# Where a weight tile's conversion keeps its scratch, and which PSUM bank takes seven of its differences

## The chip, the cores and the metric

The kernel runs on one core of a Trainium2 chip. The metric is the device time of one execution in microseconds (us): 1154.68 us is the median of three runs of the kernel before.

## The reference

Three stages follow one another, all in fp32:

```
for t in range(768):                       # 4 batches x 8 heads, head size 48
    S = a_n[t] * S + outer(k[t], v[t])     # complex decay a_n, real k and v
    y[t] = q[t] @ real(S)
x = y as [3072 tokens, 384]
x = relu(x @ w_in)**2 @ w_out                            # 384 -> 2048 -> 384
x = (silu(x @ w_gate) * (x @ w_val)) @ w_out2            # 384 -> 1536 -> 384
```

The weights come in fp32. The kernel splits every weight, and every activation that meets one, into a high part of TensorE's fp32r kind and the difference to it, and adds three products of such parts.

## The kernel before

**Stages.** The 768 steps are cut into six chunks of 128 steps (512 tokens). Chunk n goes through `attention(n)`, which forms the recurrence in closed form: `elem` does elementwise work (mostly VectorE and ScalarE), `mat` does small matmuls on TensorE, by four groups of two heads. Its result lies in `xf`, and `moe1(n)` multiplies it: for each of 16 column tiles i of 128, nine matmuls into `h` (by `w1t[i]`), ScalarE makes u = relu squared, `gh` and `gl` are its two parts, and two tiles later nine matmuls (`down`) add into three accumulators `acc0` to `acc2` (by `w2t[i]`). Meanwhile `attention(n+1)` runs. After chunk 5, `moe2` runs for all chunks.

**Weights of the first product.** `prep1` (line 815) converts 32 weight tiles, number j = 0 to 31, by turns of w_in (`wc`) and w_out (`wr`). A tile is read into a staging buffer `wst` (four of them, the slots w28 to w31), and three VectorE instructions build its high and low bits in an int32 scratch tile `wt` of 128x384 (`wsplit`, line 739). ScalarE casts `wt` into the first half of the weight tile. The second half is the difference: for j < 16 TensorE forms it in a PSUM tile `pw` (one matmul of `wt`, one of the first half with a negative identity) and ScalarE copies it out; from 16 on VectorE subtracts. Two ScalarE passes over `wst` look for values out of bounds and end the use of that staging buffer.

**Where things lie.** The 32 weight tiles have slots w0 to w31, tile j in slot j. While the first chunk's attention runs, slots 12 to 27 hold its inputs and intermediate tiles. The scratch `wt` takes a buffer of the ring `u` (three buffers), which `moe1` uses for its u too. PSUM has eight banks: three with the name `ps`, two with `h`, and one each for `acc0`, `acc1`, `acc2`. The first chunk's `mat` goes round seven of them, all but `acc2`. `pw` takes `acc2` while the flag `nc.later` is set, and a `ps` bank otherwise.

**Order.** All instructions from attention to the end are recorded first. `Plan.arrange` (line 172) then plays through them with estimated durations: whenever an engine is free it takes the ready instruction of lowest rank, which is the place in the recording (plus 1000 while `nc.later` is set). Buffers of one tag are given out in the order of their tiles' first recorded use, and a tile that isn't next in that order can't begin. The resulting list is issued (line 306, so nearly all instructions carry that line), each engine working strictly down its own list. In the recording, `drain` mixes generators by weights: during `attention(0)` one step of `prep1` goes in for every 25 steps of attention, with `later` = 1000 (line 1028); then `behind` puts two conversions ahead of each tile i of `moe1(0)` (line 1031), mixed with `attention(1)`. `attention(0)` has some 97 steps, so three conversions (j = 0 to 2) are recorded within it; j = 3 and 4 come right behind it, then u of tile 0, then j = 5 and 6, then u of tile 1, and so on.

Of the kernel before, what the change touches and what calls it, by code (L numbers as in the profile page):

```python
# [11 lines left out]
I32 = mybir.dt.int32  # L12
# [296 lines left out]
class Kern:  # L309
# [426 lines left out]
                yield  # L736


    def wsplit(self, dst, src, early=False, pe=None):

        nc = self.nc
        lo, hi = src[:, :, 0], src[:, :, 1]
        if early:
            t = self.mp.tile([128, 512], I32, name="wt", tag="u", bufs=self.NU)[:, 0:384]
        else:
            t = self.e2.tile([128, 384], I32, name="wt", tag="smk", bufs=self.NSMK)
        nc.vector.tensor_scalar(out=t, in0=hi, scalar1=3, scalar2=0x3FFFFFF8,
                                op0=ALU.logical_shift_left, op1=ALU.bitwise_and)
        nc.vector.scalar_tensor_tensor(out=t, in0=hi, scalar=-0x40000000, in1=t,
                                       op0=ALU.bitwise_and, op1=ALU.bitwise_or)  # L750
        nc.vector.scalar_tensor_tensor(out=t, in0=lo, scalar=29, in1=t,
                                       op0=ALU.logical_shift_right, op1=ALU.bitwise_or)
        x = t.bitcast(F32)
        if self.guard:
            nc.vector.tensor_scalar(out=hi, in0=hi, scalar1=0x7FFFFFFF, scalar2=None, op0=ALU.bitwise_and)
            nc.vector.scalar_tensor_tensor(out=x, in0=hi.bitcast(F32), scalar=WLOW, in1=x, op0=ALU.is_ge, op1=ALU.mult)
        nc.scalar.copy(dst[:, 0], x)
        if pe:
            pw = (self.ps if pe == "ps" else self.psa).tile([128, 384], F32, name="pw", tag=pe)
            nc.tensor.matmul(pw, self.ident, x, start=True, stop=False)  # L760
            nc.tensor.matmul(pw, self.nident, dst[:, 0], start=False, stop=True)
            nc.scalar.copy(dst[:, 1], pw)
        else:
            nc.vector.tensor_tensor(out=dst[:, 1], in0=x, in1=dst[:, 0].bitcast(F32), op=ALU.subtract)
        if not self.guard:
            hi = hi.bitcast(F32)
            nc.scalar.activation(out=hi, in_=hi, func=AF.Square, accum_out=self.flag(1))
            nc.scalar.activation(out=hi, in_=hi, func=AF.Relu, scale=-1.0, bias=self.wlow2, accum_out=self.flag(2))
# [39 lines left out]

        self.convert("wr", self.read_row(src, i), i, dst)

    def convert(self, name, st, i, dst, early=False, pe=None):
        dst[i] = t = self.wtile(name)
        self.wsplit(t.rearrange("p x k f -> p x (k f)"), st, early, pe)

    def prep1(self, ahead=0):

        self.w1t, self.w2t = {}, {}
        todo = [x for i in range(self.F1 // 128) for x in (
            (self.read_col, self.w1, i, "wc", self.w1t), (self.read_row, self.w2, i, "wr", self.w2t))]
        own = len(todo) - ahead  # L820
        read = []
        for j in range(-1, len(todo)):
            while len(read) < min(len(todo), j + max(ahead, 1)):
                f, src, i, _, _ = todo[len(read)]
                read.append(f(src, i, own + len(read) % ahead if len(read) < own and ahead else None))
            if j >= 0:
                _, _, i, name, dst = todo[j]
                self.convert(name, read[j], i, dst, ahead > 0, self.nc.later and "acc2" or "ps" if 0 < ahead and j < self.BYPE else None)
            yield

    def prep2(self):
# [377 lines left out]
```

## Time and profile before

| | |
|---|---|
| median of three runs | 1154.68 us (1154.52 to 1156.37) |
| the profiled execution: its time | 1152.95 us |
| its span, first to last instruction | 1150.8 us |
| mean granted TensorE clock | 0.984 |
| PE (matmul) busy | 1064.3 us, 92% |
| PEld (weight load) busy | 898.7 us, 78% |
| VectorE (DVE) busy | 707.5 us, 61% |
| ScalarE (ACT) busy | 617.3 us, 54% |

PE is TensorE's matmul stream, PEld its weight loads, SPq the queue that issues nearly all transfers. A row of the timeline has the start and duration in us, the engine, the line, the operation, output <- inputs, and in brackets how long the engine had been idle before it and what ended that. The span is 2.15 us shorter than the profiled execution's time, and that time is 1.73 us under the median.

### The profile page before, as it was taken

The page shows a single profiled execution, that of the slowest core. Times are in us where ns is not written, and L with a number is a line of the kernel's source. Part 1 is how long each engine was busy: PE and PEld are TensorE (multiplying, and loading weights), DVE is VectorE, ACT ScalarE, POOL GpSimd, SP SyncE. Part 2 cuts the span into 40 slices and gives each one's busy share as a digit, 9 for nine tenths or more (in the row PEclk, how much of TensorE's full clock was granted, in tenths as well). Part 3 has the DMA queues.
Part 4 walks back from the last instruction along what each step waited for, and adds up shares of the span by engine and source line. Part 5 has one row for each costly group of instructions (what it writes and reads, how often), then busy time and mean ns, then how long its engine had stood idle before and what let it go on. Part 6 is the DMA issues. An engine that isn't in the chain of part 4 may idle for free.

```text
span 1150.8 us, 16440 instructions
## 1 busy us (share of the span) xinstructions
PE 1064.3 (92%) x5890; PEld 898.7 (78%) x5890; DVE 707.5 (61%) x1485; ACT 617.3 (54%) x1334; POOL 0.9 (0%) x7
## 2 busy tenths in 40 slices
PE   2449679999999999999999999999999999999997
PEld 0347467887888888888887887888888888888886
DVE  7987999799699799789748893232232222322221
ACT  6558689966676776766759994222122222221221
POOL 0000000000000000000000000000000000000000
PEclk9969989999999999999999999999999999999998
DMA  5453346412621531531446441010010100000000
GB/s 141 129 144 96 110 149 195 110 43 75 162 68 49 153 90 50 141 85 54 137 119 190 150 148 56 1 56 1 1 55 1 55 1 1 28 1 1 28 1 31
DMA packets 102491, 89.25 MB, mean 78 GB/s; under 512 B 35073, under 2 KB 90369, under 8 KB 102401
## 3 DMA queue, kind: packets, MB, share of 16 engines
q1 hardware_dynamic: 102080, 87.93, 26.3%
q8 instruction: 48, 0.79, 0.3%
q14 instruction: 43, 0.34, 0.1%
q10 hardware_dynamic: 320, 0.20, 0.1%
HBM read 64.49 MB, written 18.87 MB: 72 GB/s over the span
## 4 chain that ended last, share of the span: by engine, by line
PE 77%; ACT 10%; DVE 7%; DMA 2%; SPq 2%; issue 2%; ACTq 0%; DVEq 0%
PE acc L306 25%; PE pg L306 13%; PE pv L306 13%; PE h L306 13%; PE py L306 4%; ACT wst L306 4%; PE pt L306 3%; PE sc L306 3%; PE pu L306 3%; SPq L306 2%; ACT u L306 1%; DVE AB L306 1%; DMA kn<-scr 1%; DVE an L306 1%; DVE wt L306 1%
## 5 line engine op out<-in xcount | busy, mean ns | idle before, releaser
L306 ACT CAST gh<-u 128x512 fp32r<-128x512 f32 x168 | 103.7, 618 | 244.4 <-PE acc L306 217.0
L306 PE MATMUL acc<-gh,wr 128*128 128x512 f32 x576 | 198.2, 400 | 4.2 <-ACT gh L306 4.1
L306 PE MATMUL h<-xh,wc 128*128 128x512 f32 x576 | 196.2, 397 | 2.7 <-ACT u L306 1.9
L306 DVE TENSOR_TENSOR gl<-u,gh 128x512 fp32r<-128x512 f32 x168 | 115.3, 688 | 126.2 <-ACT gh L306 125.7
L306 DVE TENSOR_TENSOR u<-pv,u 128x512 f32<-128x512 f32 x72 | 49.8, 692 | 204.9 <-PE pv L306 203.8
L306 PE MATMUL acc<-wr,gh 128*128 128x384 f32 x576 | 146.7, 335 | 0.0
L306 PE MATMUL pg<-xh,wc 128*128 128x512 f32 x396 | 134.8, 394 | 1.1 <-ACT xh L306 1.1
L306 PE MATMUL pv<-xh,wc 128*128 128x512 f32 x396 | 133.8, 392 | 1.3 <-ACT u L306 1.3
L306 PEld LDWEIGHTS acc<-gh,wr 128*128 128x128 f32 x576 | 107.8, 189 | 28.0 <-ACT gh L306 6.0
L306 PEld LDWEIGHTS h<-xh,wc 128*128 128x128 f32 x576 | 108.1, 189 | 26.5 <-ACT u L306 2.7
L306 PE MATMUL acc<-gl,wr 128*128 128x512 f32 x288 | 114.6, 398 | 0.2 <-DVE gl L306 0.2
L306 PE MATMUL h<-xl,wc 128*128 128x512 f32 x288 | 113.2, 393 | 0.0
L306 PEld LDWEIGHTS acc<-wr,gh 128*128 128x128 f32 x576 | 105.1, 188 | 5.2
L306 ACT ACTIVATE u<-pg 128x512 f32<-128x512 f32 x72 | 43.1, 599 | 104.7 <-PE pg L306 104.7
L306 PE MATMUL acc<-wr,gl 128*128 128x384 f32 x288 | 96.6, 335 | 0.0
L306 PEld LDWEIGHTS pv<-xh,wc 128*128 128x128 f32 x396 | 74.3, 188 | 18.3 <-ACT u L306 1.7
L306 PEld LDWEIGHTS pg<-xh,wc 128*128 128x128 f32 x396 | 74.3, 188 | 16.2 <-ACT xh L306 1.5
L306 ACT ACTIVATE u<-h 128x512 f32<-128x512 f32 x96 | 56.6, 591 | 47.3 <-PE h L306 41.7
L306 PE MATMUL pg<-xl,wc 128*128 128x512 f32 x198 | 78.2, 395 | 0.1
L306 PE MATMUL pv<-xl,wc 128*128 128x512 f32 x198 | 77.8, 393 | 0.0
L306 DVE SCALAR_TENSOR_TENSOR wt<-wst,wt 128x384 int32<-128x384 int32 x136 | 73.7, 552 | 1.6
L306 DVE TENSOR_TENSOR AB<-an 128x768 f32<-128x768 f32 x72 | 68.4, 950 | 0.7
(132 smaller groups left out, 1738.3 us busy)
## 6 DMA issues: line engine op xcount, KB each, us to landing
wst<-in_moe_w_out_dram SPq DMA_DIRECT2D x28, 384.0 KB, 3.3
scr<-ks SPq DMA_DIRECT2D x24, 384.0 KB, 2.5
kn<-scr SPq DMA_DIRECT2D x24, 384.0 KB, 3.7
wst<-in_moe_w_in_dram SPq DMA_DIRECT2D x16, 384.0 KB, 3.7
in<-in_k_dram SPq DMA_DIRECT2D x96, 48.0 KB, 1.9
in<-in_q_dram SPq DMA_DIRECT2D x96, 48.0 KB, 2.0
vt<-in_v_dram SPq DMA_DIRECT2D x48, 96.0 KB, 2.8
x2d<-x SPq DMA_DIRECT2D x18, 256.0 KB, 2.1
```

The source lines that it names most:

```text
L306: o.call(*o.args, **o.kw)
```

## The change

The scratch `wt` of tile j moves out of the ring `u` into the slot of the tile two further on (j + 2), for j + 2 below 28; the last six stay in the ring. `pw` of the first seven tiles takes the bank `acc2`, where before only those recorded under `later` did; tiles 7 to 15 stay with `ps`. `prep2`, which converts the later weights, passes no `early` and keeps its own scratch.

```diff
-    def wsplit(self, dst, src, early=False, pe=None):
+    def wsplit(self, dst, src, early=None, pe=None):
         nc = self.nc
         lo, hi = src[:, :, 0], src[:, :, 1]
-        if early:
+        if early is None:
+            t = self.e2.tile([128, 384], I32, name="wt", tag="smk", bufs=self.NSMK)
+        elif early < self.WBUFS - self.READ:
+
+            t = self.slot("wt", [128, 384], I32, early)
+        else:
             t = self.mp.tile([128, 512], I32, name="wt", tag="u", bufs=self.NU)[:, 0:384]
-        else:
-            t = self.e2.tile([128, 384], I32, name="wt", tag="smk", bufs=self.NSMK)
...
-    def convert(self, name, st, i, dst, early=False, pe=None):
+    def convert(self, name, st, i, dst, early=None, pe=None):
...
-                self.convert(name, read[j], i, dst, ahead > 0, self.nc.later and "acc2" or "ps" if 0 < ahead and j < self.BYPE else None)
+                self.convert(name, read[j], i, dst, j + 2 if ahead else None, "acc2" if j < 7 else "ps" if 0 < ahead and j < self.BYPE else None)
```

## Rows read from the trace of the kernel before

**Rows 1.** The page's parts 1 and 2: engines, then 40 slices in tenths.

```profile
PE 1064.3 (92%) x5890; PEld 898.7 (78%) x5890; DVE 707.5 (61%) x1485; ACT 617.3 (54%) x1334; POOL 0.9 (0%) x7
...
PE   2449679999999999999999999999999999999997
...
DVE  7987999799699799789748893232232222322221
```

**Rows 2.** Busy time by stretch of the span; the first row names the columns.

```profile
core 0: us, PE busy (x) PEld busy (x) DVE busy (x) ACT busy (x) POOL busy (x), PEclk, DMA share, GB/s
...
60.00:96.00 36.00, 21.00 (x164) 18.26 (x158) 29.03 (x74) 22.82 (x53) 0.00 (x0) 0.72 0.49 133
96.00:114.00 18.00, 16.94 (x68) 12.27 (x67) 15.88 (x34) 16.56 (x41) 0.00 (x0) 1.00 0.35 86
114.00:150.00 36.00, 23.30 (x84) 16.09 (x82) 35.90 (x90) 24.60 (x64) 0.00 (x0) 0.87 0.31 92
150.00:168.00 18.00, 14.81 (x85) 11.50 (x84) 16.85 (x40) 14.20 (x37) 0.00 (x0) 0.97 0.60 184
168.00:216.00 48.00, 47.58 (x375) 38.74 (x374) 41.85 (x91) 46.30 (x121) 0.00 (x0) 1.00 0.57 166
```

**Rows 3.** Waits of PE, 90 to 160 us, then 160 to 232: total, times, longest.

```profile
PE pw L306 <- DVE wt L306: 7.4, 3, 3.4
PE acc L306 <- ACT gh L306: 4.0, 2, 3.7
PE h L306 <- ACT u L306: 1.9, 2, 1.6
...
PE py L306 <- DVE rho L306: 2.9, 1, 2.9
```

**Rows 4.** Timeline: conversions 3 and 4, u of tile 0, conversions 5 and 6.

```profile
49.98 0.35 DVE L306 TENSOR_SCALAR wt<-wst 128x384 int32<-128x384 int32 x1
...
56.58 0.31 DVE L306 TENSOR_SCALAR wt<-wst 128x384 int32<-128x384 int32 x1
...
95.58 0.88 PE L306 MATMUL pw<-wt,ident 128*128 128x384 f32 x2
...
102.29 0.60 ACT L306 ACTIVATE u<-h 128x512 f32<-128x512 f32 x1 [0.62 <-PE h L306]
102.39 0.62 DVE L306 TENSOR_SCALAR wt<-wst 128x384 int32<-128x384 int32 x2
```

**Rows 5.** Stretches of tile pw: stretch, length, PE, PEld, ACT busy (count).

```profile
35.00:95.50 60.50, 0.00 (x0) 0.00 (x0) 0.00 (x0) 0.83 0.47 138
95.50:114.00 18.50, 5.79 (x17) 3.30 (x18) 2.33 (x5) 1.00 0.35 87
```

**Rows 6.** A stretch of tile wt: PE, PEld, DVE, ACT busy (count).

```profile
95.50:114.00 18.50, 4.75 (x12) 2.17 (x12) 5.00 (x12) 2.04 (x4) 1.00 0.35 87
```

**Rows 7.** Timeline: the longest two waits of DVE between 60 and 96 us.

```profile
82.34 0.56 DVE L306 SCALAR_TENSOR_TENSOR b<-sq,b 128x384 f32<-128x384 f32 x1 [0.95 <-ACT b L306]
...
89.57 0.55 DVE L306 TENSOR_TENSOR state<-pu,rho 96x384 f32<-96x384 f32 x1 [2.65 <-PE pu L306]
```

**Rows 8.** Timeline: a matmul into pw, u of tile 5 and the accumulation behind it.

```profile
136.84 0.81 PE L306 MATMUL pw<-wt,ident 128*128 128x384 f32 x2
...
139.54 0.58 ACT L306 ACTIVATE u<-h 128x512 f32<-128x512 f32 x1
...
141.48 1.65 PE L306 MATMUL acc<-gh,wr 128*128 128x512 f32 x3 [3.66 <-ACT gh L306]
```

**Rows 9.** Timeline: weight loads for pw of conversions 1 and 2, in bank acc2.

```profile
16.17 0.50 PEld L306 LDWEIGHTS pw<-wt,ident 128*128 128x128 f32 x2 [1.40 <-ACT wc L306]
...
18.99 0.50 PEld L306 LDWEIGHTS pw<-wt,ident 128*128 128x128 f32 x2 [1.67 <-ACT wr L306]
```

**Rows 10.** The SP queue's waits, 0 to 300 us: total, times, longest.

```profile
SPq L306 <- ACT wst L306: 32.7, 20, 5.0
```

**Rows 11.** The chain of waits where moe1(0) ends and moe1(1) begins.

```profile
222.79 6.12 PE acc L306 x27
228.91 6.15 PE h L306 x27
```

**Rows 12.** Timeline: the last transfers into xf of chunk 1.

```profile
215.90 1.15 SPq L306 DMA_DIRECT2D xf<-ys  x2
```

## The prediction

> **What bounds the kernel now.** I read the 40 slices first, then busy time by stretch, then who PE waited for, then the timeline where it waited. The slices show two kernels in one [rows 1]: from the seventh slice on PE is at nine tenths or more nearly to the end, and over the span it is busy 92%; in the first six slices it is not, and there VectorE is at seven to nine tenths. So only the first 170 us can give anything back by better order; whatever PE loses there is lost to the end, since all later work queues behind it. By stretch [rows 2]: from 60 to 96 us the first chunk's attention runs, PE is busy 21.0 of 36 us and DVE 29.0. From 96 to 114 moe1(0) starts, and PE is busy 16.9 of 18. From 114 to 150 PE is busy only 23.3 of 36, DVE 35.9: VectorE is the bound. From 150 to 168 PE has 14.8 of 18, and from 168 to 216 it has 47.6 of 48. PE's idle time from 96 to 168 is thus 1.1 + 12.7 + 3.2 = 17.0 us, and the waits name its causes [rows 3]: 7.4 us for scratch tiles that VectorE had not built, 4.0 for gh, 1.9 for u, 2.9 for rho of the attention.
>
> **Why the conversions are late.** Two orders of buffers hold them. Conversion 3 is built on VectorE from 49.98 us and conversion 4 from 56.58, but no matmul into pw runs between 35 and 95.5 us [rows 4, 5]; the first comes at 95.58. Its bank is of `ps`, given out in order of recording, and all of attention(0) is recorded ahead of it. Until then the scratch tiles 3 and 4 hold two of the ring's three buffers. Behind them in the ring stands u of tile 0, which begins at 102.29 when moe1(0) has its first `h`; conversions 5 and 6 come behind that u, and start 0.1 us after it, at 102.39. From there each pair of conversions is tied to the u before it, and the u to the pair before it. One case shows what that costs: u of tile 5 comes behind scratch 14 in the ring; a matmul on a scratch tile still runs at 136.84, u begins at 139.54, and PE has then sat 3.66 us waiting for the gh made from it [rows 8].
>
> **The change part by part.**
>
> *The bank.* pw of conversions 3 to 6 goes to acc2, which attention(0) never uses; no instruction is added or removed. Conversions 3 and 4 can then end some 40 us earlier, and 5 and 6 needn't wait for ps. Of PE's work, 17 matmuls into pw, 5.79 us, lie between 95.5 and 114 us [rows 5]; at three per conversion that is 5.79 / 17 x 3 = 1.02 us each, so four of them move 4.1 us into a stretch where PE has 15 us idle [rows 2]. That is worth 4.1 us if PE is the bound right after 96 and nothing if VectorE is. As VectorE is the bound from 114 on, I take nothing for it in the sum, and keep 4.1 for the upper end.
>
> *One bank for four.* The four follow one another in a single bank, so each waits for ScalarE to empty the one before. The rows of conversions 1 and 2 show that wait on PEld: 1.40 and 1.67 us [rows 9]. Queued behind such a wait on PE are attention(0)'s transposes and score matmuls, and ScalarE and VectorE wait for those. Three such waits are 3 x 1.67 = 5.0 us of PE at most; PE's 15 us of idle time hides them, and I take 0, with 5.0 as the far end if they fall just ahead of a transpose that is due.
> The Trainium skill says in Perfetto Trace Analysis, section Matmuls, that independent matmul groups should go round different PSUM banks, so that emptying one overlaps the next group's matmuls. These two rows agree that without it a group waits; by that rule the bank costs up to the 5.0 us, by the stretch's idle time it costs nothing.
>
> *The scratch.* wt of conversions 0 to 25 leaves the ring. What goes is the tie to u: conversions 5 and on can be built as soon as their read has landed and VectorE has a free moment, and u has three buffers to itself. What is added is a new order in the slots: the weight tile j + 2 can't be written before scratch j is done with. Scratch 10 and on lie in slots that attention(0) uses, so they wait for its qs, ks and kn; those end by about 96 us. So up to seven conversions (3 to 9) could be built ahead of 96 us, in place of two. What limits them is VectorE and the four staging buffers. Four conversions (5 to 8) cost VectorE 12 instructions and 5.00 us, which now lie between 95.5 and 114 us [rows 6]. Between 60 and 96 us VectorE has 36.00 - 29.03 = 7.0 us idle [rows 2], 0.95 and 2.65 us of it in two waits [rows 7]. So those 5.0 us fit. The planner puts them there by rank, behind all attention(0) work, but an engine can't break off an instruction; I take 1.0 us of delay of attention(0)'s end for that (two instructions of 0.5 us at bad moments; bounds 0 and 5.0, if every one of them delays the chain). In the DVE-bound stretch 5.0 us less of VectorE work means that PE's needs are met 5.0 us earlier.
>
> *The stalls by the ring.* 3.66 us for gh [rows 8] and 1.6 us for u [rows 3] are waits in which u came late: 5.3 us. With u free of the scratch they can go, but VectorE, busy 35.9 of 36 us there, is the next to be late, with gl and the scratch tiles. I take half, 2.65 us (bounds 0 and 5.3).
>
> *The handover.* moe1(1) takes over at 228.91 behind 6.12 us of accumulation [rows 11], and the last transfers of its input are issued at 215.90 [rows 12]. They need some microseconds to land and be split; still, about 8 us of slack stand between attention(1)'s end and PE's need. A gain of under 8 us passes even if attention(1) ends no earlier; VectorE has 48.0 - 41.9 = 6.1 us idle from 168 to 216 [rows 2] to catch up in. From there PE is the bound, and I carry the gain to the end undiminished.
>
> *Sum.* 5.0 - 1.0 + 2.65 = 6.65 us. On the profiled execution: 1152.95 - 6.65 = 1146.3 us; its time is 1.73 us under the median, so on the scale of the medians 1154.68 - 6.65 = 1148.0 us.
>
> **The rivals.**
>
> *VectorE's work is only moved (no change).* From 60 to 168 us VectorE is the chain; its gaps are waits inside that chain, and every conversion put into one could delay attention(0) by as much as it saves later. Then 5.0 - 5.0, and the freed u finds VectorE late: 1154.7, give or take 2 us. Against it: 2.65 of the 7.0 us are one wait for PE, in which four instructions fit [rows 7].
> The Trainium skill, Perfetto Trace Analysis, section Identifying the Most-Contended Engine, says to work on the engine with the highest occupancy; by that alone PE, at 92%, is the one, the change takes no instruction from it, and the time stays 1154.7. The trace agrees from 168 us on, and not from 114 to 150, where VectorE is at 35.9 of 36.
>
> *The reads stand in the way (slower).* A conversion that ends early lets the next read into its staging buffer, and the SP queue works in order: it already waits 32.7 us in 20 times for ScalarE to finish with wst, 5.0 at the longest [rows 10]. If a read of tiles 9 to 12 stands there ahead of the last groups' ks, kn or ys transfers, attention(0) ends later by that wait. Two waits of 5.0 us against the 6.65 gained give 3.4 us slower, 1158. It decides from the point where the waits ahead of those transfers exceed 6.65 us. Against it: the planner counts the read's readiness before it places it.
>
> *All stalls go (more).* If conversions stay ahead of moe1(0) for good, the 17.0 us of PE's idle time [rows 2] shrink to little, and the 4.1 us of pw count too: 21.1 us at most. Half to all of that gives 1133.6 to 1144. For it: VectorE has 7.0 us idle before 96 and 6.1 after 168. Against it: it has 0.1 between 114 and 150, and attention(1) must end earlier by what exceeds the 8 us of slack.
>
> **How the numbers follow.** Forecast, 3 to 10.5 us gained: 0.55, at 1148.0, own range 1144 to 1152. More than that: 0.15. No change: 0.16. Reads in the way or another slowing: 0.14. A measurement of this kernel tells about 0.2% (2.3 us) from no change. Faster 0.70, same 0.16, slower 0.14. The range for 8 in 10 goes from 1138, within the rival with more, to 1157, within the slower one.
>
> **What the trace after would show.** Right: pw matmuls of conversions 3 to 6 and scratch tiles 5 to 8 ahead of 95 us; attention(0)'s last transfer into xf within 2 us of where it was; PE's idle time from 96 to 168 at about 10 us in place of 17; PE's start of moe1(1) 5 to 9 us earlier and no new gap after it. Wrong: VectorE as idle before 96 as now; moe1(0)'s first h later by as much as the stalls shrink; SP waits for wst ahead of ks, kn or ys; or a new wait of PE at 220 us for xf of chunk 1.

## The result, and the profile after

The change is faster: 1144.95 us, the median of six runs (1144.47 to 1146.38), against 1155.48 for the kernel before on the same chip (six runs, 1153.10 to 1156.85). The ratio is 0.9913, with a 95% interval of 0.9900 to 0.9926, or 10.0 us (the two medians differ by 10.5). The forecast was 1148.0 us and 6.65 us of gain, the range 1138 to 1157: sign and mechanism hold, the gain was half as large again. Between the two profiled executions it is 1152.95 - 1144.72 = 8.2 us; the profiled execution of before lies 2.5 us under the median of its runs, that of after 0.2. The traces can explain only those 8.2.

The page of after, engines and slices, answers to [rows 1]:

```profile
PE 1067.2 (93%) x5890; PEld 899.9 (79%) x5890; DVE 705.8 (62%) x1485; ACT 619.3 (54%) x1334; POOL 1.0 (0%) x7
...
PE   2458979999999999999999999999999999999997
...
DVE  6998999799789789789658883232232222322221
```

No instruction went or came: the counts are those of before, and over the span no engine is busier by more than 3 us. What changed is when the work is done. Busy time by stretch, in the columns of [rows 2] (length, PE, PEld, DVE, ACT, POOL, granted clock, DMA share, GB/s):

```profile
60.00:96.00 36.00, 23.92 (x151) 17.70 (x151) 32.35 (x85) 28.91 (x74) 0.00 (x0) 0.72 0.52 141
96.00:114.00 18.00, 14.83 (x68) 10.64 (x68) 17.43 (x37) 15.64 (x37) 0.00 (x0) 0.81 0.54 146
114.00:150.00 36.00, 30.15 (x131) 24.12 (x129) 35.19 (x89) 27.49 (x67) 0.00 (x0) 0.95 0.33 95
150.00:168.00 18.00, 15.65 (x89) 12.71 (x90) 17.73 (x41) 13.55 (x33) 0.00 (x0) 0.81 0.57 170
168.00:216.00 48.00, 47.60 (x368) 38.66 (x367) 41.11 (x87) 45.99 (x117) 0.00 (x0) 1.00 0.55 157
```

VectorE's idle time ahead of 96 us fell from 7.0 to 3.65 us. PE's idle time from 96 to 168 fell from 17.0 to 3.2 + 5.8 + 2.4 = 11.4 us; it fell by 6.9 us between 114 and 150, where VectorE was the bound and still is, and grew by 2.1 ahead of 114. The waits of PE from 96 to 240 us (total, times, longest) show what is left:

```profile
PE pt L306 <- DVE ks L306: 8.2, 1, 8.2
PE h L306 <- ACT xh L306: 2.4, 1, 2.4
PE h L306 <- ACT u L306: 0.8, 1, 0.8
PE h L306 <- DVE xl L306: 0.7, 1, 0.7
```

All the causes of [rows 3] are gone: the 7.4 us for scratch, 4.0 for gh, 2.9 for rho, and most of the u. Two waits have come in their place, 8.2 us for ks, the scaled k of attention(1), and 2.4 for xh, the high part of moe1(0)'s input (0.8 before). The timeline of after, in order of time (start, duration, engine, line, operation, idle time before it):

```profile
57.94 0.81 PE L306 MATMUL pw<-wt,ident 128*128 128x384 f32 x2
...
62.03 0.35 DVE L306 TENSOR_SCALAR wt<-wst 128x384 int32<-128x384 int32 x1
...
64.74 1.65 PE L306 MATMUL pw<-wt,ident 128*128 128x384 f32 x2 [1.56 <-ACT wr L306]
...
67.28 1.65 PE L306 MATMUL pw<-wt,ident 128*128 128x384 f32 x2 [0.57 <-ACT wc L306]
...
77.36 0.62 DVE L306 TENSOR_SCALAR wt<-wst 128x384 int32<-128x384 int32 x2
...
97.97 0.57 ACT L306 ACTIVATE ys<-py 48x512 f32<-48x512 f32 x1
...
101.72 0.52 SPq L306 DMA_DIRECT2D xf<-ys  x1
...
104.60 0.62 ACT L306 CAST xh<-xf 128x512 fp32r<-128x512 f32 x1 [0.19 <-DMA xf<-ys]
...
105.27 0.93 PE L306 MATMUL h<-xh,wc 128*128 128x512 f32 x2 [2.43 <-ACT xh L306]
...
152.35 1.09 PE L306 MATMUL pt<-ident,ks 128*96 128x128 f32 x4 [8.20 <-DVE ks L306]
...
221.81 0.39 PE L306 MATMUL h<-xh,wc 128*128 128x512 f32 x1
```

The pw of conversion 3 now runs at 57.94 us, not at 95.58 [rows 4]; conversion 5 begins on VectorE at 62.03, not at 102.39, 7 and 8 at 77.36, and 9 at 83.99. In one bank, two of the pw groups wait for ScalarE, 1.56 and 0.57 us, as in [rows 9]. Then the bill: the last two ys of attention(0), 0.7 us apart, come 2.7 us later than before (the first of them at 97.97 for 95.25; that one is meant by "the last ys" below), the last transfer into xf is issued at 101.72 (before, the last two from 97.04 within 1.16 us, so the last at about 97.6), and the last cast into xh 4.5 us later (104.60 for 100.12). moe1(1) begins at 221.81, for 228.75 before. Two rows on the tiles pw (PE, PEld, ACT busy) and wt (PE, PEld, DVE, ACT busy) of after:

```profile
35.00:95.00 60.00, 7.10 (x12) 3.01 (x12) 1.92 (x4) 0.83 0.47 137
...
35.00:96.00 61.00, 5.72 (x8) 1.81 (x8) 9.89 (x21) 3.04 (x6) 0.83 0.48 139
```

Twelve matmuls into pw, four differences, where [rows 5] has none. 21 VectorE instructions on scratch are seven conversions, 3 to 9, where before there were two in 2.86 us: five more, and 7.0 us of VectorE's time moved ahead.

The gain can be balanced on PE from 60 us to the start of moe1(1). The two long rows of before, and then those of after:

```profile
96.00:168.00 72.00, 55.05 (x234) 39.86 (x233) 68.63 (x162) 55.36 (x138) 0.00 (x0) 0.93 0.39 113
168.00:228.75 60.75, 60.33 (x431) 49.25 (x430) 51.23 (x108) 58.21 (x147) 0.00 (x0) 1.00 0.55 154
```

```profile
96.00:168.00 72.00, 60.63 (x286) 47.46 (x286) 70.36 (x164) 56.69 (x134) 0.00 (x0) 0.88 0.44 126
168.00:221.81 53.81, 53.41 (x394) 43.45 (x392) 45.38 (x95) 51.43 (x129) 0.00 (x0) 1.00 0.53 151
```

With the 15.0 and 12.1 us of idle time ahead of 96, PE idles 15.0 + 16.95 + 0.42 = 32.4 us before and 12.1 + 11.37 + 0.40 = 23.9 after, 8.5 less; it is busy 136.4 and 138.0 us, 1.6 more at a lower clock. 8.5 - 1.6 is the 6.9 us by which moe1(1) starts earlier. Chunk 1 adds 2.0 (its idle time falls from 3.0 to 0.9 us). In the chain of waits moe1(2) and moe1(4) then begin here, against 330.61 and 525.54 before:

```profile
321.65 6.12 PE h L306 x27
...
517.38 6.12 PE h L306 x27
```

That is 9.0 and 8.2 us earlier, and 8.2 it is at the end.

### The profile page after: what moved, and what is told of

The parts are those of the page before. It is cut to its first block, busy times and chain, and to the rows that moved or that the text cites. A ratio compares the mean times of both kernels' runs of the same rounds, so it can differ in the third digit from the quotient of the medians.

```text
span 1142.6 us, 16426 instructions
## 1 busy us (share of the span) xinstructions
PE 1067.2 (93%) x5890; PEld 899.9 (79%) x5890; DVE 705.8 (62%) x1485; ACT 619.3 (54%) x1334; POOL 1.0 (0%) x7
## 4 chain that ended last, share of the span: by engine, by line
PE 79%; ACT 9%; DVE 6%; DMA 2%; SPq 2%; issue 1%; ACTq 0%; DVEq 0%
PE acc L306 26%; PE h L306 13%; PE pg L306 13%; PE pv L306 13%; PE py L306 4%; ACT wst L306 3%; PE pt L306 3%; PE sc L306 3%; PE pu L306 3%; SPq L306 2%; ACT u L306 2%; DVE an L306 1%; DMA wst<-in_moe_w_in_dram 1%; DVE AB L306 1%; ACT gh L306 1%
## 5 line engine op out<-in xcount | busy, mean ns | idle before, releaser
L306 PE MATMUL h<-xh,wc 128*128 128x512 f32 x576 | 199.2, 400 | 3.2 <-ACT xh L306 2.4
L306 PE MATMUL acc<-gh,wr 128*128 128x512 f32 x576 | 195.7, 396 | 0.1
```

What stands on the lines that cost most here:

```text
L306: o.call(*o.args, **o.kw)
```

## The experiments

Each ratio is to the kernel before on the same chip, with its 95% interval.

**The scratch alone.** The change without its bank.

```diff
-..., "acc2" if j < 7 else "ps" if 0 < ahead and j < self.BYPE else None)
+..., self.nc.later and "acc2" or "ps" if 0 < ahead and j < self.BYPE else None)
```

> Only the scratch moves to the later tile's slot; the differences keep the banks of before (acc2 for the first three, ps after). My theory (the head start of conversions 3 to 9 and the cut tie to u together): conversions 3 to 9 are still built on VectorE ahead of 96 us, but their seven differences of some 1.02 us each all run behind attention(0); the gain is that of the change (10 us by the medians) less the 4.1 us of TensorE work that stays: ratio 0.994 to 0.997, and no matmul into pw between 35 and 95 us. Rival (the bank makes the gain, since it lets the chain of conversions begin): ratio 0.998 to 1.002.

Measured: 0.9937 (0.9925 to 0.9949), 1146.97 against 1154.74 us. The stretches of pw (PE, PEld, ACT), and then PE's longest wait from 96 to 240:

```profile
35.00:95.00 60.00, 0.00 (x0) 0.00 (x0) 0.00 (x0) 0.86 0.49 143
95.00:114.00 19.00, 8.04 (x24) 4.08 (x24) 2.79 (x6) 1.00 0.56 154
```

```profile
PE pt L306 <- DVE ks L306: 12.6, 1, 12.6
```

VectorE does the same seven conversions early (9.86 us on wt ahead of 96), but no difference is formed, and 24 matmuls into pw, 8.04 us, stand between 95 and 114 us. The scratch carries about 0.63 of the 0.87%, a little more than the 0.3 to 0.6% that were expected.

**The bank alone.** The kernel before, with the bank of the change.

```diff
-..., ahead > 0, self.nc.later and "acc2" or "ps" if 0 < ahead and j < self.BYPE else None)
+..., ahead > 0, "acc2" if j < 7 else "ps" if 0 < ahead and j < self.BYPE else None)
```

> Only the bank: the first seven differences in acc2, the scratch in the ring u as before. My theory: conversions 3 and 4 end early, but 5 and 6 still begin right behind u of tile 0 (at about 102 us), so at most 2.0 us of TensorE work moves: ratio 0.998 to 1.000. Rival (the bank makes the gain): ratio 0.991 to 0.995.

Measured: 1.0002 (0.9992 to 1.0011): no change. PE's waits:

```profile
PE pw L306 <- DVE wt L306: 7.3, 3, 3.4
PE acc L306 <- ACT gh L306: 4.0, 2, 3.7
...
PE h L306 <- ACT xh L306: 2.1, 1, 2.1
```

The first two are those of [rows 3]; the wait for xh was 0.8 us before. Six pw matmuls (3.19 us) run early, but the last ys comes at 98.03, 2.8 us later than before, with no conversion moved ahead (2.85 us on wt before 96 us, as in the kernel before). With the scratch alone it comes at 96.38, 1.1 us later. So most of the delay of that ys belongs to the early pw, not to VectorE's early work. At the last cast into xh, which moe1(0) needs, it is the other way round: 102.56 with the bank alone, 104.30 with the scratch alone, for 100.12 before and 104.60 with both. What the scratch adds behind that ys is found below, with the transfers. Alone the bank buys nothing, since conversions 5 and on are still tied to u; on top of the scratch the ratio goes from 0.9937 to 0.9913. Those two intervals just touch, and a mere change of order moves the time by 0.14% (below), so the 0.24% is not certain.

**The tie put back for conversions 5 to 8.** No head start, but u and scratch apart from conversion 9 on.

```diff
-..., j + 2 if ahead else None, ...
+..., (99 if 5 <= j < 9 else j + 2) if ahead else None, ...
```

> The change, but conversions 5 to 8 keep their scratch in the ring u, behind u of tiles 0 and 1; 9 and on have it in the later tile's slot. This takes away the head start and leaves the cut tie from conversion 9 on. If the cut tie makes the gain: ratio 0.990 to 0.994, attention(0) ends as early as before (its last ys at 95 to 96 us, in place of 98). If the head start makes it: ratio 0.997 to 1.000.

Measured: 0.9966 (0.9955 to 0.9978). PE's waits:

```profile
PE acc L306 <- DVE gl L306: 7.6, 2, 5.8
PE pw L306 <- DVE wt L306: 3.1, 3, 2.0
PE h L306 <- ACT xh L306: 2.1, 1, 2.1
```

The 4.0 us for gh are gone, those for scratch fall from 7.4 to 3.1, and gl, which VectorE makes, takes 7.6 in their place.

**The tie put back from conversion 9 on.** The head start alone.

```diff
-..., j + 2 if ahead else None, ...
+..., (j + 2 if j < 9 else 99) if ahead else None, ...
```

> The change, but conversions 9 and on keep their scratch in the ring u; 3 to 8 have it in the later tile's slot. This leaves the head start and the tie to u from tile 3 on. If the head start makes the gain: ratio 0.990 to 0.994, with attention(0)'s last ys at about 98 us. If the cut tie makes it: ratio 0.997 to 1.002, and PE waits for scratch or gh of 3 us and more between 120 and 150 us come back.

Measured: 0.9944 (0.9931 to 0.9957). PE's waits:

```profile
PE h L306 <- ACT wc L306: 6.7, 1, 6.7
PE acc L306 <- ACT gh L306: 5.9, 2, 3.2
```

The waits for gh are back with the tie. Each expectation set a reading in which the one half makes the gain against one in which the other does; both ratios lie between, so each half has a share. The halves, 0.34% (cut tie) and 0.56% (head start), add up to 0.90%, about the whole 0.87%.

**Less VectorE work.** The change without the second of the three VectorE instructions for the scratch of the 32 tiles of w_in and w_out, so that the two top bits of each weight's high part are left out.

```diff
-        nc.vector.scalar_tensor_tensor(out=t, in0=hi, scalar=-0x40000000, in1=t,
-                                       op0=ALU.bitwise_and, op1=ALU.bitwise_or)
+        if early is None or self.guard:
+            nc.vector.scalar_tensor_tensor(out=t, in0=hi, scalar=-0x40000000, in1=t,
+                                           op0=ALU.bitwise_and, op1=ALU.bitwise_or)
```

> The changed kernel without one of the three VectorE instructions that build each scratch tile of the first product's weights (it leaves out the two top bits of the high part): 32 x 0.47 us = 15 us of VectorE less, no other engine's work changed. Theory (VectorE still bounds the stretch up to 168 us after the change): some 20 of these lie ahead of 168 us, 9 us; the wait of PE of 8.2 us for ks shrinks to 3 us or less and the ratio to the kernel before falls from 0.991 to 0.983 to 0.987. Rival (what is left is the planner's order and the transfers, not VectorE's load): 0.989 to 0.992.

Measured: 0.9854 (0.9837 to 0.9871), 1139.28 against 1156.14 us; from 35 to 216 us VectorE spends 33.4 us on wt, for 48.2 in the change. PE's longest wait:

```profile
PE pt L306 <- DVE ks L306: 10.5, 1, 10.5
```

The total says that VectorE is still what bounds these stages: less of its work is less time. The wait was to shrink to 3 us or less, and it grew to 10.5. The time came back elsewhere: the wait for xh is 0.6 us, and moe1(1) begins at 217.36, some 4.4 us ahead of the change. In the change's own wait for ks, 8.2 us long, only one of VectorE's 19 instructions, of 0.34 us, belongs to a conversion; the others are attention(1)'s. One wait doesn't measure its cause; where PE catches up with VectorE depends on the order.

**The last transfers taken out of SP's line.** The change, with the last group's xf transfers of chunk 0 on ScalarE's queue.

```diff
-                        nc.sync.dma_start(out=xf[row % 128:row % 128 + m, row // 128],
+                        q = nc.scalar if n == 0 and g == 3 else nc.sync
+                        q.dma_start(out=xf[row % 128:row % 128 + m, row // 128],
```

> The changed kernel, with the last group's transfers into xf of the first chunk issued from ScalarE's queue and not from SP's. Theory (in the changed kernel the end of attention(0) is late by some 2 us because these transfers stand behind others in SP's order): xh of the last part begins 4.2 us behind the last ys, as before the change, in place of 5.9, and the ratio falls by 0.0015 to 0.989 to 0.991. Rival (VectorE and PE have other work meanwhile): 0.991 to 0.993 and no change.

Measured: 0.9896 (0.9881 to 0.9911). The interval overlaps that of the change, so the two aren't told apart. The timeline:

```profile
98.08 0.60 ACTq L306 DMA_DIRECT2D xf<-ys  x1
...
98.91 0.51 ACTq L306 DMA_DIRECT2D xf<-ys  x1
...
104.16 0.63 ACT L306 CAST xh<-xf 128x512 fp32r<-128x512 f32 x1
```

The transfers are issued 1.8 and 2.8 us earlier (99.83 and 101.72 in the change), the cast comes only 0.4 earlier, at 104.16, and PE's wait for xh is 2.4 us as before. What was won at the issue was lost up to the landing: the two took 5.0 and 4.6 us to land, for 4.3 and 2.8 in the change and 2.3 and 2.4 in the kernel before. In the change the DMA engines are full then. From 96 to 102 us, the kernel before and then the change (the last two columns are the DMA share and GB/s):

```profile
96.00:102.00 6.00, 5.16 (x21) 3.51 (x20) 5.55 (x12) 4.88 (x11) 0.00 (x0) 1.00 0.56 124
...
96.00:102.00 6.00, 6.00 (x45) 4.85 (x45) 5.43 (x12) 5.68 (x15) 0.00 (x0) 1.00 0.99 306
```

Most of that is four reads into wst of 384 KB each, issued between 94.98 and 97.54 us; the kernel before issues none there. SP's queue waits for such reads to land as well (the change, 80 to 106 us; before has no such wait there):

```profile
SPq L306 <- DMA wst<-in_moe_w_in_dram: 0.9, 1, 0.9
SPq L306 <- DMA wst<-in_moe_w_out_dram: 0.7, 2, 0.4
```

So this run takes the transfers out of SP's line, but not out of the way of the reads, which the early conversions let go. All the runs agree: counting reads into wst issued from 6 us ahead of the last ys on, from that ys to the last cast into xh it takes 4.5 to 5.4 us in the four kernels without such reads (before, before reordered, the bank alone, and the tie put back for 5 to 8), and 5.9 to 7.9 in the nine with two to four of them. Only the last 0.7 us here, from the landing at 103.50 to the cast, are left to ScalarE's own list. No run holds the reads back, so what they cost in time stays open.

**Three conversions ahead.** The change, with three conversions ahead of each tile of moe1(0) in the recording.

```diff
-            for _ in range(2):
+            for _ in range(3):
```

> The changed kernel with three conversions recorded ahead of each tile of moe1(0) in place of two, so that they rank earlier against attention(1). Theory (after the change conversions 16 and on are late because VectorE takes attention(1)'s work first): moe1(0) runs longer before PE's first long wait, attention(1)'s ks comes later, and with VectorE as the bound the sum is the same: ratio 0.990 to 0.994. Rival (the tie was the whole limit, more head start gives more): ratio below 0.989.

Measured: 1.0013 (1.0003 to 1.0023); a gain of 0.6 to 1.0% was expected, so this was missed. PE's waits, and the stretches from 114 us:

```profile
PE acc L306 <- DVE gl L306: 14.3, 2, 13.5
PE h L306 <- ACT u L306: 7.1, 2, 6.5
```

```profile
114.00:150.00 36.00, 23.30 (x102) 18.54 (x100) 35.11 (x86) 26.18 (x68) 0.00 (x0) 0.87 0.32 96
150.00:168.00 18.00, 10.16 (x51) 7.89 (x51) 18.00 (x41) 11.52 (x31) 0.00 (x0) 0.88 0.74 210
```

Nearly nine conversions (26 instructions) are done ahead of 96 us, VectorE is as full as ever, and PE starves: a gl of moe1(0) starts on VectorE only at 150.02, and VectorE waited for others just 0.5 us from 114 to 168, so gl stood behind other work in its list. moe1(1) begins at 238.94, 17.1 us after the change's. The edit does more than lengthen the head start from seven conversions to nine: it puts all later conversions earlier in the recording too. So it shows that conversions can come too early, and not what two more of them ahead of 96 us would do alone.

**How much is order alone.** The planner's estimate of one DMA issue, 475 ns for 470, in the kernel before and in the change: the same program in another order.

```diff
-            return 470, 2000 + 4 * free.ap[0][1] * self.width(free) / 250.0
+            return 475, 2000 + 4 * free.ap[0][1] * self.width(free) / 250.0
```

> The kernel before with one estimate of the planner changed: a transfer's issue costs 475 and not 470 ns. No instruction is added, removed or retied; only ties in the order can fall another way. It shows how far the time moves by reordering alone. Theory (differences of over 0.3% between the runs here are not chance of ordering): ratio 0.998 to 1.002. Rival (the list is that sensitive): outside it.

> The changed kernel with the planner's one estimate 475 in place of 470 ns for a transfer's issue, nothing else. If the order behind the change is robust: ratio 0.989 to 0.9935. If a good part of the 0.9913 is a lucky order: 0.994 or more.

Measured: 0.9986 (0.9973 to 0.9999) of before, and 0.9918 (0.9897 to 0.9940) for the change reordered. A change of order moves the time by some 0.1% (1.6 us); the gain is not of that kind. But the second one's waits are others: 6.5 us for a weight tile of VectorE in place of most of the wait for ks (1.3 left). The total is steady, the place of the wait isn't.

**Half of the head start.** Conversions 7 and 8 go back into the ring.

```diff
-..., j + 2 if ahead else None, ...
+..., (99 if 7 <= j < 9 else j + 2) if ahead else None, ...
```

> The change, but conversions 7 and 8 keep their scratch in the ring u behind u of tile 1; 5 and 6, and 9 and on, have it in the later tile's slot. Half of the head start is left. Theory (the gain of the head start follows from VectorE's work moved ahead of 96 us, about 1.4 us per conversion less the delay of attention(0)): ratio halfway between the kernel without the head start (0.9966) and the change (0.9913), 0.9925 to 0.9955. Rival (beyond 5 and 6 the head start only delays attention(0)): 0.991 or below.

Measured: 0.9933 (0.9912 to 0.9954), about halfway between none (0.9966) and all (0.9913), with five conversions early (7.12 us, 15 instructions). The interval reaches far enough toward either end that the middle is not sharp.

**More differences on PE.** The change, with conversions 16 to 23 also forming their difference on PE, and not on VectorE.

```diff
-    BYPE = 16
+    BYPE = 24
```

> The changed kernel with the differences of tiles 16 to 23 formed on TensorE too, as those of 0 to 15 are. VectorE loses 8 x 0.47 = 3.8 us, TensorE gets 8 x 1.02 = 8.2 us and ScalarE 8 copies of 0.48 us. Theory (VectorE is the bound up to 168 us, TensorE from there on; these tiles are converted between 150 and 190 us): most of TensorE's 8.2 us come behind 160 us and are paid in full, VectorE's part is gained back partly: 2 to 7 us slower than the change, ratio 0.993 to 0.998. Rival (VectorE bounds moe1(0) to its end): 0.986 to 0.991.

Measured: 0.9947 (0.9931 to 0.9962), 0.34% slower than the change. All the added matmuls come behind 150 us, where PE has little time to spare (busy 16.90 of 18 us up to 168, then 48.00 of 48 up to 216), and PE's wait for ks, which is nearly over by then, is 9.3 us: VectorE's relief comes too late for the stretch that needs it.

## Why the prediction was right, and where its sizes were off

*Head start, 5.0 less 1.0: right, too small.* Against the kernel with conversions 5 to 8 tied (0.9966) the whole change (0.9913) gains 0.53%, 6.1 us, with the bank's part in it. The term counted four conversions, though the same passage has up to seven ahead in place of two, and five more came ahead: 7.0 us of VectorE's time in place of 5.0. Their work fitted because VectorE's idle time went from 7.0 to 3.65 us, and the rest pushed attention(0)'s own work back.

*The delay of attention(0), 1.0 us: too small: two causes were put at nothing.* It was 2.7 us at the last ys, 4.1 at the last transfer into xf (forecast: within 2) and 4.5 at the last xh. At that ys VectorE's early work costs 1.1 us, as the term had it (scratch alone, 96.38). The rest has two causes. One is the step "I take 0, with 5.0 as the far end" for the one bank: early pw alone delays that ys by 2.8 us (98.03). How much of this is the wait for the bank (1.56 us there) and how much PE's time for the differences (3.19 us) no run separates, and the two delays don't add (97.97 with both). The other is the reads into wst, which the sum left to a rival: of the 4.5 us at xh, 2.7 come with ys, about 1.4 in SP's queue, which waits 0.4 and 0.9 us for reads into wst to land, and 0.4 by a slower landing.

*The bank, 0: perhaps too small.* Alone it is nothing, as the sum had it. With the scratch it is about 0.24%, or 2.8 us, inside the bound of 4.1, if it is real. The reason given for 0 was that VectorE is the bound from 114 us on. A reading that would fit, argued and not tried: PE idles and works by turns there, and work that it needn't do at 96 to 114 us lets moe1(0) be further on when the wait comes; then the step took an average bound for a bound at each instant. The Trainium skill, in Perfetto Trace Analysis, section Matmuls, asks for separate groups to go round several banks; here the one bank has its waits (1.56 and 0.57 us), and still the change is not slower than the scratch alone, which leaves these differences to the banks `ps` (0.9913 against 0.9937); from 60 to 96 us PE has 12 us idle.

*The stalls by the ring, 2.65 us: near.* The cut tie is 0.34% alone and 0.31% on top of the head start (0.9944 to 0.9913), 3.6 to 3.9 us. The waits for u and gh go with it and come back with it. What the forecast said is late next, gl and the scratch tiles, is late in the run without head start; in the change it is ks.

*The idle time: about 10 us forecast, 11.4 found,* and not spread: 8.2 of it is one wait, which the forecast didn't name. It did say what bounds: VectorE is busy in all of those 8.2 us (below).

*The handover: right.* moe1(1) starts 6.9 us earlier, within 5 to 9, no new gap of more than 0.8 us follows, and the slack held.

*Rivals.* That VectorE's work is only moved falls with the interval. That the reads stand in the way came true in part: reads that the early conversions let go stand before the last transfers into xf, but they cost xh up to 1.8 us (1.4 and 0.4, above), less than the 6.65 us from which that rival decides. That all stalls go: the time lies in the forecast's own range (1144 to 1152), at the edge next to that rival's; 11.4 of the 17.0 us are still there.

## What to carry to other kernels

Where a producer's scratch comes out of the same ring as its consumer's tiles, the order of the ring is a wait that no engine's busy share shows; give the scratch buffers of its own, those of later outputs where none are free. A bank freed alone does nothing while another buffer still holds the same work back, so such changes are judged together. Filler that goes into idle time on an engine that works strictly down its list also delays that engine's critical work, here the last ys by 1.1 us for VectorE's filler and by 2.7 with PE's; and it sets free the next reads, which can stand before small transfers that the critical work needs.

## What the runs showed that was not expected

A wait of PE can cost more than its length. Busy time by short stretches of after, the first around the wait for xh, the second around that for ks (the column behind POOL is the granted clock):

```profile
106.00:110.00 4.00, 3.26 (x8) 2.15 (x7) 4.00 (x10) 3.61 (x8) 0.00 (x0) 0.50 0.26 49
110.00:114.00 4.00, 4.00 (x14) 3.11 (x13) 4.00 (x8) 3.35 (x9) 0.00 (x0) 0.69 0.03 6
...
144.10:152.30 8.20, 0.05 (x1) 0.00 (x0) 8.20 (x19) 4.08 (x8) 0.00 (x0) 0.65 0.20 49
152.30:156.00 3.70, 3.65 (x13) 2.84 (x14) 3.70 (x10) 1.56 (x3) 0.00 (x0) 0.50 0.30 118
156.00:160.00 4.00, 4.00 (x32) 3.83 (x31) 3.73 (x9) 3.28 (x10) 0.00 (x0) 0.90 0.39 124
```

Behind both waits the granted clock is 0.50, the 1.2 GHz level, and then rises. As an estimate, busy time times the missing share of the clock: behind the 8.2 us it costs 3.65 x 0.50 + 4.00 x 0.10 = 2.2 us of PE's time, behind the 2.4 us (and 0.7 for xl soon after) it costs 3.26 x 0.50 + 4.00 x 0.31 = 2.9 us, about as much as the waits themselves. Before, the stretch from 96 to 114 us had a granted clock of 1.00 [rows 2]. The forecast counted idle time only. By the same estimate, taken by half microseconds from 96 to 168 us, the kernel before loses 3.1 us and the change 5.3; the 2.2 us between them are near the 1.6 by which PE was busier in the balance above. The Trainium skill describes such a fall behind waits for transfers in TensorE: Matmul & The Clock Gate, section HAM oscillation; here it comes behind waits for ScalarE and VectorE.
